# Moving weight loads, row loads, splits and sums to other places in a fused attention and expert kernel

## The chip, the cores and the metric

The kernel runs on one core of one Trainium2 chip. The metric is the time of one execution on the device, in microseconds (us).

## What is computed

A recurrent attention over 32 heads (4 batches of 8) gives x, 3072 rows of 384 numbers. Each row then goes to the best two of eight experts, weighted by its gate:

```python
for e in range(E):
    for k in range(2):
        mask = top2[:, k] == e
        if not mask.any():
            continue
        h = np.maximum(x[mask] @ w1[e], 0.0)
        out[mask] += top2_w[mask, k, None] * (h @ w2[e])
```

`w1[e]` is 384x1024 and `w2[e]` is 1024x384, all in 32-bit floats.

## The kernel before

**Attention and gating** come first, in six groups of 512 rows. Their steps and the steps of the first two experts are calls with names. The text `EMIT` sets the order in which the calls are written, and the table `ORDER` sets by hand the order of their instructions on each engine: PE (matmul), ACT, DVE, POOL, and SP, whose queue issues the plain DMAs. A token such as `load_w20.2` is the third instruction of one call on one engine. In names, `mm10_0_5` is the first product of the first expert, first half of its rows, sixth block of hidden units; `load_w10` and `load_w11` load the first weights of the first and of the second expert, `load_w20` the second weights of the first expert, `load_x1_0` the first half of the second expert's rows. At the end of gating each row is scattered by POOL into `xs`, a DRAM tensor with one stretch for each expert.

**The experts** are ranked by their number of rows. The largest two are computed in the hand-ordered part; the other six in a loop, `for e in range(2, E)`, where e is the rank. In the loop there is no table: the program text, a scheduler and the dependencies named `order` set the order, and SP's DMAs stay in the order of the text.

One expert's turn has these pieces. Half `w=0` has 256 to 320 rows ("narrow"), half `w=1` has 512 ("wide").

- `mm1(e, w)`: for each of eight blocks f of 128 hidden units, nine matmuls into one of four PSUM buffers `ph`. ACT then writes the rounded high part of relu (line 933, list `highs`), DVE the rest (line 936, list `lows`). We call these two the eviction of block f. A buffer is free after both.
- `mm2(e, w)`: hidden units times `w2` into one of two PSUM buffers `po`; DVE adds the weighted result to `ao` (line 980, list `kept`), POOL scatters `ao` into the output. For e of 2 to 5 the first half is computed turned (`mm2_turned`): it goes through the DRAM tensor `op`, comes back by a transposing DMA (`turn_back`, line 1001), and is added (`add_turned`, lines 1008 and 1011) in the turn of the next expert.
- Weights: a load into one of three `raw` buffers (lines 861 and 870), then a split in a high part by ACT and a low part by DVE (line 851). `w1` comes in three loads, `w2` in four; the fourth `w2` load needs a `raw` buffer that a split has emptied.
- Rows of the next expert: `load_x` brings them into `xga` (first half) and `xgb` (second), `x_G` reads out the gates on DVE, `x_P` copies the halves of each word apart on ACT (line 816) and stores them in `xp`, `x_L` reads them back with twelve transposing DMAs of SP (line 825), and `x_T` copies (DVE, line 910), rounds (ACT, line 913) and subtracts (DVE, line 914).
- `gather_o`: POOL reads the output rows into `ao` before they are added to.

The tile `xp0` serves both `x_P` of the first half and the turned product on its way to `op`; `xp1` serves `x_P` of the second half and the turned sums on their way back. An engine runs its instructions in their order: one that waits holds all behind it.

Of the kernel before, what the change touches and what calls it, by code (L numbers as in the profile page):

```python
# [71 lines left out]
    tr_unit22_0 p3q23_1 load_x1_0 sc_unit21_0 st_scale17 x_unit19 tr_unit22_1 sc_unit21_1 y_unit21 tr_unit23_0  # L72
    gdis4_3_4 sc_unit22_0 st_scale18 sc_unit22_1 tr_unit23_1 st_scale19 y_unit22 sc_unit23_0 load_v23 sc_unit23_1
    gscat4_3_4 glog5_0_3 x_unit20 gturn5_0_3 mm10_0_5 gsel5_0_3 mm10_0_6 y_unit23 gdis5_0_3 mm10_0_0 mm10_0_3 x_unit21
    mm10_0_7 mm10_0_4 close_q load_w20 load_w11 x_T1_0_0 glog5_3_4 x_T1_0_1 gturn5_3_4 x_unit22 gscat5_0_3 gsel5_3_4
    x_unit23 x_T1_0_2 gdis5_3_4 rank gscat5_3_4 x_G1_0 clear_out3 clear_mp mm20_0_0 mm20_0_1 mm20_0_2 mm11_0_0
    mm11_0_1 mm11_0_2 load_x0_1 mm11_0_3 mm11_0_4 mm11_0_5 mm11_0_6 x_G0_1 x_T0_1_0 x_T0_1_1 mm11_0_7 x_T0_1_2
    mm10_1_0 mm10_1_1 mm10_1_2 load_x1_1 x_P1_1 x_L1_1 mm10_1_3 mm10_1_4 mm10_1_5 mm10_1_6 mm10_1_7 ranked load_w12
    x_T1_1_0 load_x2_0 x_T1_1_1 mm20_1_3 mm20_1_4 x_G1_1 x_T1_1_2 x_P2_0 x_L2_0 x_G2_0 mm20_1_5 load_x2_1 mm20_1_6
    x_P2_1 x_L2_1 x_G2_1 load_w21 mm11_1_0 mm11_1_1 mm11_1_2 mm11_1_3 mm11_1_4 gather_o1 mm11_1_5 mm21_0_0 mm11_1_6  # L80
    mm21_0_1 mm11_1_7 x_T2_0_0 x_T2_0_1 x_T2_0_2 mm21_0_2 mm21_1_3 x_T2_1_0 x_T2_1_1 x_T2_1_2 mm21_1_4 mm21_1_5
    mm21_1_6
# [119 lines left out]
        gdis4_0_3.2 gdis4_0_3.1 sc_unit22_0.0 gsel4_3_4.16 gdis4_0_3.3 load_w20.0 sc_unit22_1.0 load_w20.2 st_upd15.0  # L202
        st_scale19.0 gdis4_3_4.0 gdis4_3_4.1 sc_unit23_1.0 sc_unit23_0.0 load_w20.1 gturn5_0_3.0 gsel5_0_3.0
        gsel5_0_3.1 gsel4_3_4.13 load_w20.3 gsel5_0_3.2 gsel5_0_3.3 mm10_0_5.0 gsel5_0_3.4 gsel5_0_3.5 gsel5_0_3.6
        mm10_0_5.1 gsel5_0_3.9 gsel4_3_4.14 gsel5_0_3.8 gsel5_0_3.7 gsel5_0_3.12 gsel5_0_3.11 mm10_0_6.0 mm10_0_6.1
        gsel5_0_3.14 gsel5_0_3.15 gsel5_0_3.10 gsel5_0_3.13 gsel5_0_3.16 gsel5_0_3.20 gdis4_3_4.2 mm10_0_0.0
        gsel4_3_4.15 gsel5_0_3.17 gdis4_3_4.3 gsel5_0_3.18 mm10_0_0.1 gdis5_0_3.0 gsel5_0_3.19 gdis5_0_3.2 mm10_0_3.0
        mm10_0_3.1 gdis5_0_3.3 gdis5_0_3.1 x_T1_0_0.0 mm10_0_7.0 gturn5_3_4.0 gsel5_3_4.0 x_T1_0_1.0 gsel5_3_4.1
        gsel5_3_4.2 gsel5_3_4.3 gsel5_3_4.4 gsel5_3_4.5 gsel5_3_4.6 mm10_0_7.1 mm10_0_4.0 gsel5_3_4.7 gsel5_3_4.10
        gsel5_3_4.8 mm10_0_4.1 gsel5_3_4.11 gsel5_3_4.9 gsel5_3_4.12 gsel5_3_4.13 load_w11.0 gsel5_3_4.14 gsel5_3_4.16  # L210
        x_T1_0_2.0 gsel5_3_4.15 rank.1 gdis5_3_4.0 gdis5_3_4.2 gdis5_3_4.3 clear_mp.0 clear_mp.4 load_w11.2 load_w11.1
        gdis5_3_4.1 rank.0 rank.2 clear_mp.3 clear_mp.2 clear_mp.1 clear_mp.5 rank.3 mm20_0_1.0 mm20_0_0.0 mm11_0_2.0
# [111 lines left out]
def kernel(  # L324
# [468 lines left out]
    def load_x(e, w, dst):  # L793
# [14 lines left out]
    XU = {}  # L808
    after = mybir.DependencyInfo(mybir.DependencyClass.NoSync, mybir.DependencyReason.DATA)

    def x_P(e, w):
# [3 lines left out]
        for i in range(len(js)):  # L815
            nc.scalar.copy(t[:, i], src_t[:, i, 0:DM].bitcast(U16).rearrange("p (d two) -> p two d", two=2))
# [450 lines left out]
    for e in range(2, E):  # L1267
# [5 lines left out]
        else:  # L1273
            for f2 in range(RAW):
                split_w2(f2)
# [206 lines left out]
```

## Time and profile before

| | |
|---|---|
| time, three runs | 667.25 us median (666.02 to 670.16) |
| the profiled execution | 667.93 us, its span 666.2 us |
| PE busy | 642.0 us, 96% of the span |
| DVE busy | 433.1 us, 65% |
| ACT busy | 366.7 us, 55% |
| POOL busy | 177.7 us, 27% |
| granted clock of PE, mean | 0.995 |

The span goes from the first to the last instruction that the profiler saw; the execution has 1.7 us around it. All durations below are from this one execution. Busy time of PE counts a matmul to its modelled end, so a busy PE may still be slower than its peak; idle time of PE is certain.

### The profile page before, as it was taken

The numbers are of one execution on the slowest core, as the hardware profiler recorded it, in microseconds if no ns is written. First come the engines' busy times: TensorE is split into PE (matmuls) and PEld (weight loads), VectorE is DVE, ScalarE is ACT, GpSimd is POOL, SyncE is SP. The second block draws the span as 40 slices with busy tenths as digits, with TensorE's granted clock in tenths as the row PEclk, the third lists the DMA queues.
The fourth block names the chain that finished last, engine by engine and source line by source line (L and its number), as shares of the span: only waits on it lengthen the run. The fifth ranks groups of instructions, "written<-read, shape, count | busy, mean of one in ns | idle before, by whom it ended". The sixth has DMA issues, their size and how long they took to land.

```text
span 666.2 us, 14314 instructions
## 1 busy us (share of the span) xinstructions
PE 642.0 (96%) x5511; PEld 568.9 (85%) x5514; DVE 433.1 (65%) x976; ACT 366.7 (55%) x609; POOL 177.7 (27%) x183
## 2 busy tenths in 40 slices
PE   7889999999999899999999999999998998999995
PEld 3467787878899799898998999999898898899894
DVE  6999999999999576455566167347427607827311
ACT  6999999999855452545237227326415515604200
POOL 3000000065524551036224023412411602523111
PEclk9999999999999999999999999999999999999998
DMA  6946756667595842686629467768766677772111
GB/s 236 302 136 165 214 148 225 207 212 234 184 276 175 295 178 99 241 242 175 180 85 341 77 192 240 184 176 267 174 163 216 185 185 206 216 196 84 45 37 36
DMA packets 117901, 123.75 MB, mean 186 GB/s; under 512 B 71498, under 2 KB 96992, under 8 KB 117824
## 3 DMA queue, kind: packets, MB, share of 16 engines
q1 hardware_dynamic: 108560, 95.27, 48.6%
q0 software_dynamic: 9264, 27.48, 12.8%
q8 instruction: 45, 0.74, 0.5%
q14 instruction: 32, 0.26, 0.1%
HBM read 70.11 MB, written 42.90 MB: 170 GB/s over the span
## 4 chain that ended last, share of the span: by engine, by line
PE 68%; ACT 10%; DMA 8%; SPq 7%; DVE 4%; issue 2%; POOL 0%; POOLq 0%; DVEq 0%; ACTq 0%
PE ph L931 21%; PE po L967 20%; SPq L825 5%; PE ptr L584 5%; PE psc L594 4%; PE po L992 3%; PE pY L643 2%; PE pY L645 2%; PE cum L534 2%; DMA xgb<-xs 2%; PE cum L561 2%; ACT t L468 2%; PE pG L606 2%; PE psc L931 2%; DMA op<-xp 2%
## 5 line engine op out<-in xcount | busy, mean ns | idle before, releaser
L931 PE MATMUL ph<-x,w1h 128*128 128x512 f32 (+4 forms) x720 | 185.2, 345 | 3.3 <-DVE h L936 3.2
L967 PE MATMUL po<-w2h,h 128*128 128x384 f32 x640 | 164.9, 335 | 0.8 <-DVE ao L980 0.8
L931 PEld LDWEIGHTS ph<-x,w1h 128*128 128x128 f32 x720 | 125.1, 188 | 19.2 <-DVE h L936 4.1
L952 POOL DMA_INDIRECT out_dram<-ao,ox x54 | 59.1, 1094 | 263.8 <-DVE ao L980 190.6
L931 PE MATMUL ph<-x,w1l 128*128 128x512 f32 (+4 forms) x360 | 124.0, 344 | 0.0
L967 PEld LDWEIGHTS po<-w2h,h 128*128 128x128 f32 x640 | 115.8, 188 | 1.7 <-DVE ao L980 1.4
L933 ACT ACTIVATE h<-ph 128x512 fp32r<-128x512 f32 (+4 forms) x120 | 60.0, 508 | 91.0 <-PE ph L931 78.5
L936 DVE SCALAR_TENSOR_TENSOR h<-ph,h 128x512 fp32r<-128x512 f32 (+5 forms) x128 | 68.5, 547 | 62.9 <-ACT h L933 62.6
L967 PE MATMUL po<-w2l,h 128*128 128x384 f32 x320 | 107.0, 334 | 0.0
L716 POOL DMA_INDIRECT xs<-xr,sl x48 | 58.3, 1215 | 178.0 <-DMA ecol<-es 129.4
L980 DVE SCALAR_TENSOR_TENSOR ao<-po,gw,ao 128x384 f32<-128x384 f32 (+1 forms) x42 | 25.7, 614 | 93.4 <-PE po L967 93.3
L931 PEld LDWEIGHTS ph<-x,w1l 128*128 128x128 f32 x360 | 67.6, 188 | 7.8 <-DVE w1l L851 0.2
L943 POOL DMA_INDIRECT ao<-out_dram,ox x47 | 52.4, 1115 | 32.6 <-issue 24.2
L967 PEld LDWEIGHTS po<-w2l,h 128*128 128x128 f32 x320 | 60.1, 188 | 0.2
L913 ACT CAST x<-xj 128x512 fp32r<-128x512 f32 (+4 forms) x39 | 20.6, 529 | 69.1 <-DVE xj L910 67.9
L914 DVE TENSOR_TENSOR x<-xj,x 128x512 fp32r<-128x512 f32 (+4 forms) x39 | 22.6, 578 | 31.0 <-ACT x L913 31.0
L594 PE MATMUL psc<-qT,kT 112*64 112x128 f32 (+1 forms) x768 | 38.9, 249 | 0.5 <-ACT kT L585 0.5
L594 PEld LDWEIGHTS psc<-qT,kT 112*64 112x64 f32 x768 | 35.8, 137 | 3.8 <-issue 2.6
L992 PE MATMUL po<-h,w2h 128*128 128x272 f32 (+2 forms) x192 | 38.7, 294 | 0.0
L645 PE MATMUL pY<-am,v 128*48 128x128 f32 x384 | 36.0, 273 | 0.2 <-DVE am L595 0.2
L595 DVE TENSOR_TENSOR am<-psc,mask 128x512 f32<-128x512 f32 x48 | 32.4, 681 | 4.0 <-PE psc L594 4.0
L851 DVE TENSOR_TENSOR w2l<-raw,w2h 128x768 fp32r<-128x768 f32 x32 | 30.3, 951 | 6.9 <-ACT w2h L851 6.9
(242 smaller groups left out, 1096.9 us busy)
## 6 DMA issues: line engine op xcount, KB each, us to landing
raw<-in_moe_w_dram SPq DMA_DIRECT2D x24, 512.0 KB
raw<-in_moe_w_dram SPq DMA_DIRECT2D x32, 384.0 KB
qk<-in_qk_dram SPq DMA_DIRECT2D x24, 384.0 KB
v<-in_v_dram SPq DMA_DIRECT2D x24, 288.0 KB
xgb<-xs SPq DMA_DIRECT2D x8, 800.0 KB
xp<-xp SPq DMA_DIRECT2D x7, 768.0 KB
re<-in_a_dram SPq DMA_DIRECT2D x12, 384.0 KB
im<-in_a_dram SPq DMA_DIRECT2D x12, 384.0 KB
```

The costliest lines, as they stand in the source:

```text
L584: nc.tensor.transpose(p[:, h, :], x[:, h, :, :].rearrange("p r x -> p (r x)")[:, 0:112], ident)
L594: nc.tensor.matmul(p[o:o + 64, j, z:], KT[n][:, h, z:z + 64], QT[n][:, h, z:], start=True, stop=True, skip_group_check=True)
L645: nc.tensor.matmul(o, V[n][:, H + h // 2 if h % 2 else h, :], AM[n][:, h, :], start=not g, stop=True, skip_group_check=True)
L716: d = nc.gpsimd.indirect_dma_start(out=xs, out_offset=bass.IndirectOffsetOnAxis(ap=sl[:, kk, b:b + 1], axis=0), in_=XR[g][:, lo + b, :], i ...
L825: nc.sync.dma_start(x[:, i, :], xp[e % 2, lo:lo + n, i * DM + kk * 128:i * DM + (kk + 1) * 128], transpose=True)
L931: nc.tensor.matmul(p[:, :n], W1[e, kk][i][:, f * 128:(f + 1) * 128], XW[w, kk][:, j, :], start=(c == 0), stop=(c == len(ms) - 1))
L933: highs.append(nc.scalar.activation(h[:, 0:n], p[:, :n], AF.Relu))
L936: d = nc.vector.scalar_tensor_tensor(h[:, dst:dst + b - a], p[:, a:b], 0.0, h[:, a:b].bitcast(F32), op0=OP.max, op1=OP.subtract)
L943: nc.gpsimd.indirect_dma_start(out=ao[j][0:w, :], out_offset=None, in_=out, in_offset=bass.IndirectOffsetOnAxis(ap=OX[e][0:w, j:j + 1], ax ...
L952: d = nc.gpsimd.indirect_dma_start(out=out, out_offset=bass.IndirectOffsetOnAxis(ap=OX[e][0:n, j:j + 1], axis=0), in_=a, in_offset=None, b ...
L967: nc.tensor.matmul(p[:, :DM], HT[w, f][i][:, o:o + 128], W2[f // 2][k2][:, f % 2, :], start=(m == 0), stop=(m == len(ms) - 1))
L992: nc.tensor.matmul(p[:, :n], W2[f // 2][k2][:, f % 2, kk * 128:(kk + 1) * 128], HT[0, f][i][:, 0:n], start=(m == 0), stop=(m == len(ms) - 1))
```

## The change

Three things change; the matmuls and their order on PE stay as they are.

1. **At the end of attention**, three of the four loads of the first expert's second weights (`load_w20_0_1_2`) stand on SP's queue ahead of two stores to `xd` and of the second expert's rows; the fourth (`load_w20_3`) stays behind the rows. The splits keep their places on ACT and DVE.
2. **Loads in the loop.** The next expert's rows are loaded ahead of the fourth `w2` load and of the `w1` loads. The store and the transposes of the first half are issued between `w1` loads, ahead of the second half's store.
3. **Work between evictions in the loop.** For e from 3 on, the first three `w2` splits move from the end of the turn before to places behind the second, fourth and sixth narrow eviction, the fourth behind the first wide one. `x_P` of the first half comes behind the sixth to eighth narrow eviction and of the second half behind the fourth wide one (for e=2 one copy behind each of the first four), the `w1` splits behind the fifth to seventh wide one. The last third of `x_T` (second half, last 128 columns) moves from the end of the turn before to behind the first narrow eviction. The turned sums come behind the first to third wide eviction.

The core of the diff (the table rows only rename `load_w20` except on SP):

```diff
@@ ORDER, SP
-        load_x0_0.0 load_x0_0.1 p322.2 p321.2 load_v20.0 load_v21.0 load_v22.0 p322.1 gscat3_0_4.0 gscat4_0_3.0
-        load_x1_0.0 load_x1_0.1 load_w20.0 load_w20.1 load_w20.2 load_v23.0 load_w20.3 load_w11.0 load_w11.1
+        load_x0_0.0 load_x0_0.1 p322.2 p321.2 load_v20.0 load_v21.0 load_v22.0 p322.1 load_w20_0_1_2.0
+        load_w20_0_1_2.1 load_w20_0_1_2.2 gscat3_0_4.0 gscat4_0_3.0 load_x1_0.0 load_x1_0.1 load_v23.0 load_w20_3.0
...
-    def x_P(e, w):
+    def x_P(e, w, part=None):
...
-        t = mt([128, len(js), 2, DM], U16, name=f"xp{w}")
-        for i in range(len(js)):
-            nc.scalar.copy(t[:, i], src_t[:, i, 0:DM].bitcast(U16).rearrange("p (d two) -> p two d", two=2))
-        nc.sync.dma_start(xp[e % 2, js[0] * 128:(js[-1] + 1) * 128].rearrange("(j p) r -> p j r", p=128),
+        if not part:
+            XP[w] = mt([128, len(js), 2, DM], U16, name=f"xp{w}")
+        t = XP[w]
+        for i in range(len(js)) if part is None else (part,):
+            d = nc.scalar.copy(t[:, i], src_t[:, i, 0:DM].bitcast(U16).rearrange("p (d two) -> p two d", two=2))
+            if e > 2:
+                tc.add_manual_dep(d.ins, highs[i - 3 if w == 0 else -1].ins.name, after, reason="order")
+        if part in (None, len(js) - 1):
+            nc.sync.dma_start(xp[e % 2, js[0] * 128:(js[-1] + 1) * 128].rearrange("(j p) r -> p j r", p=128),
...
+    def raw_w1(e, kk):
+        r = RW1[kk] = mt([128, FF], F32, name="raw", bufs=RAW)
+        nc.sync.dma_start(r, of(w1, e)[kk * 128:(kk + 1) * 128, :])
+
+    def split_w1(e, kk, behind=None):
+        W1[e, kk] = [mt([128, FF], F32R, name=f"w1{x}{kk}{e % 2}") for x in "hl"]
+        split(RW1[kk], *W1[e, kk], behind)
...
-    def load_w2(e):
-        for f2 in range(KF // 2):
+    def load_w2(e, fs=range(KF // 2)):
+        for f2 in fs:
...
-                tc.add_manual_dep(t.ins, kept[-1].ins.name, after, reason="order")
+                tc.add_manual_dep(t.ins, (lows[-KF] if (w, kk) == (1, KD - 1) else kept[-1]).ins.name, after, reason="order")
...
     def add_turned(e, y):
-        for j, first in zip(tiles_of(e, 0), lows[-3:] if e + 2 < E else lows[-6:]):
+        for j, first in zip(tiles_of(e, 0), lows[-KF:]):
...
-    at(P["w2"] + .5, load_w2, 0)
+    at(P["w2"] + .5, load_w2, 0, tuple(range(RAW)))
+    at(P["w2"] + .5, load_w2, 0, (RAW,))
...
         mm1(e, 0)
+        if more:
+            load_x(e + 1, 0, xga)
+            load_x(e + 1, 1, xgb)
         if e > 2:
+            x_T(e, 1, KD - 1)
+            for f2 in range(RAW):
+                split_w2(f2, 2 * f2 + 1 - KF)
             raw_w2(e, RAW)
-            split_w2(RAW, -4)
+        if more:
+            for kk in range(KD - 1):
+                raw_w1(e + 1, kk)
+            x_G(e + 1, 0)
+            x_P(e + 1, 0)
+        for f in range(KF):
+            mm1(e, 1, (f,))
+            if f == 0:
+                if e > 2:
+                    split_w2(RAW, -1)
+                if more:
+                    raw_w1(e + 1, KD - 1)
+                    x_L(e + 1, 0)
+                    x_G(e + 1, 1)
+            if more and f < len(JS[1]):
+                x_P(e + 1, 1, f)
+            if more and f == len(JS[1]) - 1:
+                x_L(e + 1, 1)
+            if more and f >= len(JS[1]) and f < len(JS[1]) + KD:
+                split_w1(e + 1, f - len(JS[1]), -1)
         if e - 1 in FLIP:
             add_turned(e - 1, y)
...
-                for w, kk in {3: ((0, 0), (0, 1)), 4: ((0, 2), (1, 0)), 5: ((1, 1),), 6: ((1, 2),)}[j]:
+                for w, kk in {3: ((0, 0), (0, 1)), 4: ((0, 2), (1, 0)), 5: ((1, 1),), 6: ()}[j]:
```

On SP's queue at the end of attention, in the kernel before (`xd` stores of two groups, the second expert's rows into `xga`, then the first expert's second weights; an ISA row sets the address):

```order
L713 DMA xd<-xr_2052 128x4x392
L713 DMA xd<-xr_2634 128x3x392
L796 ISA
L796 DMA xga_94<-xs 128x800
L798 ISA
L798 DMA xga_94<-xs 64x400
L870 ISA
L870 DMA raw_3722<-in_moe_w2_dram 128x2x384
```

Here the weights come last. The same place of SP's queue now:

```order
L882 DMA raw_3722<-in_moe_w2_dram 128x2x384
L882 ISA
L882 DMA raw_3728<-in_moe_w2_dram 128x2x384
L882 ISA
L882 DMA raw_3734<-in_moe_w2_dram 128x2x384
L714 DMA xd<-xr_2052 128x4x392
L714 DMA xd<-xr_2634 128x3x392
L797 ISA
L797 DMA xga_94<-xs 128x800
```

The three loads now stand ahead of the stores and rows.

On ACT, first product of expert e=5 (`h00` to `h07` are its narrow evictions, `h10` the first wide one; `w2h0` a split's high part, `x12` the last third of `x_T`, `xp0` a copy of `x_P`), in the kernel before:

```order
L851 CAST w2h2_6593<-raw_6352 128x768
L933 ACTIVATE h00_6597<-ph_6598 128x272
L913 CAST x12_6580<-xj_6581 128x512
L933 ACTIVATE h01_6610<-ph_6611 128x272
L816 COPY xp0_6875<-xga_94 128x768
L933 ACTIVATE h02_6623<-ph_6624 128x272
L816 COPY xp0_6875<-xga_94 128x768
L933 ACTIVATE h03_6636<-ph_6637 128x272
L933 ACTIVATE h04_6649<-ph_6650 128x272
L851 CAST w2h3_6703<-raw_6701 128x768
```

Here the first three splits are done ahead of the evictions, and the copies come early. The same place of ACT now:

```order
L949 ACTIVATE h01_6593<-ph_6594 128x272
L857 CAST w2h0_6691<-raw_6348 128x768
L929 CAST x12_6686<-xj_6687 128x512
L949 ACTIVATE h02_6606<-ph_6607 128x272
L949 ACTIVATE h03_6619<-ph_6620 128x272
L857 CAST w2h1_6695<-raw_6350 128x768
L949 ACTIVATE h04_6632<-ph_6633 128x272
L949 ACTIVATE h05_6645<-ph_6646 128x272
L857 CAST w2h2_6699<-raw_6352 128x768
L819 COPY xp0_6714<-xga_94 128x768
L949 ACTIVATE h06_6658<-ph_6659 128x272
L819 COPY xp0_6714<-xga_94 128x768
```

The copies from `xga` moved from behind the second narrow eviction to behind the sixth, the splits in among the evictions.

On SP's queue between the turn of e=4 and that of e=5 (`xp1` returns the turned product; `xga`, `xgb` are rows for e=6), in the kernel before:

```order
L1001 DMA_TRANSPOSE xp1_6436<-op 128x3x384 x2
L870 ISA
L870 DMA raw_6701<-in_moe_w2_dram 128x2x384
L796 ISA
L796 DMA xga_94<-xs 128x800
L805 ISA
L805 DMA xgb_3900<-xs 128x1600
```

Here the rows come behind the weights. The same place of SP's queue now:

```order
L1017 DMA_TRANSPOSE xp1_6436<-op 128x3x384 x2
L797 ISA
L797 DMA xga_94<-xs 128x800
L806 ISA
L806 DMA xgb_3900<-xs 128x1600
L882 ISA
L882 DMA raw_6703<-in_moe_w2_dram 128x2x384
```

The rows moved ahead of the fourth `w2` load.

## Rows read from the trace of the kernel before

**Rows 1.** Page, busy time: engine, us, share of the span, instructions.

```profile
PE 642.0 (96%) x5511; PEld 568.9 (85%) x5514; DVE 433.1 (65%) x976; ACT 366.7 (55%) x609; POOL 177.7 (27%) x183
```

**Rows 2.** Engines by stretch: stretch, length, busy us (instructions) of each, clock, DMA.

```profile
220.00:240.00 20.00, 17.84 (x210) 16.60 (x209) 12.66 (x56) 9.35 (x20) 10.07 (x9) 1.00 0.75 261
...
488.00:542.00 54.00, 51.86 (x314) 48.28 (x312) 28.07 (x51) 22.95 (x39) 15.41 (x14) 1.00 0.68 187
542.00:596.00 54.00, 52.10 (x299) 48.54 (x299) 29.41 (x54) 20.97 (x36) 16.30 (x15) 1.00 0.72 205
...
650.00:666.20 16.20, 8.02 (x47) 7.70 (x45) 1.59 (x3) 0.00 (x0) 2.92 (x3) 0.81 0.11 37
```

**Rows 3.** What PE waited for, 200 to 667 us: total, times, longest.

```profile
PE ph L931 <- DVE h L936: 3.2, 3, 1.3
PE cum L662 <- ACT xr L654: 1.3, 1, 1.3
PE cum L662 <- ACT xT L646: 0.8, 1, 0.8
PE po L967 <- DVE ao L980: 0.8, 2, 0.5
```

**Rows 4.** PE in order of time, 206 to 252 us: start, us, [idle before <- releaser].

```profile
225.93 0.41 PE L662 MATMUL cum<-xT,wg 128*32 128x128 f32 x4 [1.34 <-ACT xr L654]
227.16 1.06 PE L662 MATMUL cum<-xT,wg 128*32 128x128 f32 x20 [0.82 <-ACT xT L646]
```

**Rows 5.** ACT in order of time, 195 to 240 us.

```profile
224.66 0.83 ACT L851 CAST w2h<-raw 128x768 fp32r<-128x768 f32 x1 [2.66 <-DMA raw<-in_moe_w_dram]
```

**Rows 6.** SP's queue in order of time, 180 to 235 us.

```profile
198.53 13.14 SPq L713 DMA_DIRECT2D xd<-xr  x2
...
213.74 1.83 SPq L870 DMA_DIRECT2D raw<-in_moe_w_dram  x3
...
221.67 0.37 SPq L870 DMA_DIRECT2D raw<-in_moe_w_dram  x1
```

**Rows 7.** DVE in order of time, 195 to 252 us.

```profile
201.32 1.22 DVE L851 TENSOR_TENSOR w1l<-raw,w1h 128x1024 fp32r<-128x1024 f32 x1
```

**Rows 8.** ACT in order of time, 485 to 515 us.

```profile
494.24 0.83 ACT L816 COPY xp<-xga 128x768 uint16<-128x768 uint16 x1 [8.48 <-DMA op<-xp]
...
506.64 0.39 ACT L933 ACTIVATE h<-ph 128x272 fp32r<-128x272 f32 x1
509.63 0.83 ACT L816 COPY xp<-xga 128x768 uint16<-128x768 uint16 x1 [2.60 <-DMA xga<-xs]
```

**Rows 9.** PE in order of time, 488 to 512 us.

```profile
507.92 0.52 PE L931 MATMUL ph<-x,w1h 128*128 128x272 f32 x2 [1.03 <-DVE h L936]
```

**Rows 10.** SP's queue in order of time, 450 to 515 us.

```profile
494.28 2.85 SPq L1001 DMA_TRANSPOSE xp<-op  x2
503.37 0.39 SPq L870 DMA_DIRECT2D raw<-in_moe_w_dram  x1
503.95 0.36 SPq L796 DMA_DIRECT2D xga<-xs  x1
```

**Rows 11.** DVE in order of time, 485 to 515 us.

```profile
502.40 0.94 DVE L851 TENSOR_TENSOR w2l<-raw,w2h 128x768 fp32r<-128x768 f32 x1
```

**Rows 12.** Chain that ended last, whole span: start us, us, what.

```profile
381.64 16.65 PE po L967 x96
...
566.61 16.62 PE ph L931 x72
```

**Rows 13.** ACT in order of time, 270 to 345 us.

```profile
275.67 3.02 ACT L816 COPY xp<-xgb 128x768 uint16<-128x768 uint16 x4
```

**Rows 14.** POOL in order of time, 552 to 612 us.

```profile
576.00 1.07 POOL L943 DMA_INDIRECT ao<-out_dram,ox  x1 [2.54 <-issue]
```

**Rows 15.** DVE in order of time, 555 to 590 us.

```profile
571.72 0.60 DVE L1011 SCALAR_TENSOR_TENSOR ao<-xj,gw,ao 16x384 f32<-16x384 f32 x1
...
587.45 0.62 DVE L980 SCALAR_TENSOR_TENSOR ao<-po,gw,ao 128x384 f32<-128x384 f32 x1 [2.86 <-PE po L967]
```

More of the change, by code (lines that the diff above doesn't have):

```diff
@@ L71 @@
     mm10_0_1 st_scale16 y_unit20 tr_unit21_0 p3q21_1 mm10_0_2 tr_unit21_1 gdis4_0_3 gscat4_0_3 x_G0_0 p3q23_0
[L72 to L80, printed above, removed]
@@ L83 @@
+    mm21_0_0 mm11_1_6 mm21_0_1 mm11_1_7 x_T2_0_0 x_T2_0_1 x_T2_0_2 mm21_0_2 mm21_1_3 x_T2_1_0 x_T2_1_1 x_T2_1_2
+    mm21_1_4 mm21_1_5 mm21_1_6
 """
@@ L157 @@
+        x_P2_1.2 mm11_1_6.0 x_T2_0_0.0 x_T2_0_1.0 mm11_1_5.0 mm21_0_2.0 mm11_1_7.0 x_T2_0_2.0 x_T2_1_0.0 x_T2_1_1.0
+        x_T2_1_2.0
     """,
@@ L223 @@
+        x_T2_0_1.0 x_T2_0_1.1 mm21_0_1.0 mm11_1_2.0 mm11_1_6.0 mm21_0_2.0 mm11_1_5.0 x_G2_1.1 x_T2_0_2.0 x_T2_0_2.1
+        x_G2_1.2 mm11_1_7.0 mm21_0_2.1 x_T2_1_0.0 x_T2_1_0.1 x_T2_1_1.0 mm21_1_3.0 x_T2_1_1.1 mm21_1_4.0 mm21_1_5.0
+        x_T2_1_2.0 x_T2_1_2.1 mm21_1_6.0
     """,
@@ L859, in load_w1 @@
         for kk in range(KD):
-            r = mt([128, FF], F32, name="raw", bufs=RAW)
-            nc.sync.dma_start(r, of(w1, e)[kk * 128:(kk + 1) * 128, :])
-            W1[e, kk] = [mt([128, FF], F32R, name=f"w1{x}{kk}{e % 2}") for x in "hl"]
-            split(r, *W1[e, kk], 1 + 2 * kk - KF if e > 2 else None)
-    RW = {}
+            raw_w1(e, kk)
+            split_w1(e, kk)
+    RW, RW1 = {}, {}
     def raw_w2(e, f2):
@@ L889, in x_G @@
         t = chosen[:, 8 * E:(8 + len(js)) * E].rearrange("p (j e) -> p j e", e=E)
-        nc.vector.tensor_mul(t, src_t[:, 0:len(js), DM:DM + E], ONE[e][:, None, :].to_broadcast([128, len(js), E]))
+        d = nc.vector.tensor_mul(t, src_t[:, 0:len(js), DM:DM + E], ONE[e][:, None, :].to_broadcast([128, len(js), E]))
+        if e > 2:
+            tc.add_manual_dep(d.ins, lows[(-3, -1)[w]].ins.name, after, reason="order")
         nc.vector.tensor_reduce(GW[e][:, js[0]:js[-1] + 1], t, axis=AX.X, op=OP.add)
-        nc.vector.tensor_copy(OX[e][:, js[0]:js[-1] + 1], src_t[:, 0:len(js), RNO])
+        d = nc.vector.tensor_copy(OX[e][:, js[0]:js[-1] + 1], src_t[:, 0:len(js), RNO])
+        if e > 2:
+            tc.add_manual_dep(d.ins, lows[(-3, -1)[w]].ins.name, after, reason="order")
     def x_T(e, w, kk):
@@ L1270 @@
             held.close()
+        more = e + 1 < E
         if e == 2:
             load_w2(e)
-        else:
-            for f2 in range(RAW):
-                split_w2(f2)
-        if e == 2:
             for i in range(2):
@@ L1286 @@
         gather_o(e)
-        if e + 1 < E:
-            load_x(e + 1, 0, xga)
-            load_x(e + 1, 1, xgb)
-        mm1(e, 1)
-        if e + 1 < E:
-            load_w1(e + 1)
-            for w in range(2):
-                x_G(e + 1, w)
-                x_P(e + 1, w)
-            for w in range(2):
-                x_L(e + 1, w)
-        if e + 1 < E:
+        if more:
             for f2 in range(RAW):
```

84 lines of the change are left out of this document (44 added, 40 removed), and 2 rows, old and new, of the table PACE.

## The prediction

> **What bounds the kernel now.** I read the page first: PE is busy for 642.0 us, 96% of the span [rows 1]. All other engines are far below, and the change leaves every matmul in its place, so it can give back only time in which PE stands idle. The table of stretches says where that is: 2.16 us between 220 and 240 us (20.00 less 17.84), 2.14 us between 488 and 542, 1.90 us between 542 and 596, and 8.18 us at the end, where the last sums and scatters run out behind the last matmul [rows 2]. The rest of the idle time lies in the first 200 us, whose order the change doesn't touch. The list of PE's waits after 200 us names the same amount: 1.3 and 0.8 us in the gate's matmul, three waits of 3.2 us for a free `ph`, two of 0.8 us for a free `po`, 6.1 us in all [rows 3]. Up to 6.2 us is therefore the prize. Each wait has to be followed back to what made it.
>
> *The waits at 224 us.* PE's gate matmuls of line 662 wait 1.34 us for ACT's copy of `xr` and 0.82 us for its copy of `xT` [rows 4]. ACT is late because a split of `load_w20` stands ahead of those copies in its order and waits 2.66 us for its load, until 224.66 us [rows 5]. That load was issued between 213.74 and 215.57 us, since SP's queue sat in the two stores to `xd` from 198.53 to 211.67 us and then issued the second expert's rows [rows 6].
>
> *The waits for `ph`, e=5 and e=6.* PE waits 1.03 us at 507.92 us for an eviction [rows 9]. The evictions need ACT, and ACT, after its second narrow one at 506.64 us, stands 2.60 us in a copy from `xga` whose load is still on its way [rows 8]. SP issued that load at 503.95 us, right behind the fourth `w2` load at 503.37, although its queue had nothing to issue from 497.13 us on (494.28 plus 2.85) [rows 10]. A second wait in the same place and one of 1.3 us at e=6 make the 3.2 us.
>
> *The waits for `po`.* One of the three copies of `x_P` stands ahead of the casts of `x_T` on ACT and waits 8.48 us, until 494.24 us, since its tile `xp0` is still being stored to `op` [rows 8]. The casts, DVE's subtractions and DVE's eviction of `po` queue up behind it; PE loses 0.3 us there and 0.5 us in the next turn [rows 3].
>
> **The change part by part.**
>
> *Loads at the end of attention.* Three `raw` buffers are free when DVE's last split of the first expert's first weights ends, at 202.5 us (201.32 plus 1.22) [rows 7]; the last of the three loads is thus issued at about 202.6 us instead of 215.6. The casts stood between 9.1 and 10.9 us behind the issue of the late load (224.66 less 215.57 and less 213.74) [rows 5, 6]; even so the last would land at 213.5 us, over 6 us ahead of the first use. What the loads are moved past: the `xd` stores, which only the program's fallback reads, and the second expert's rows, which are issued right behind 211.67 us as before, since the second store sets that, and have fewer bytes beside them. ACT no longer waits, and both waits go: 2.16 us. Late next would be the fourth load, issued at 221.67 us when the first split has emptied its buffer [rows 6]; its cast stands behind the gate's next step and would come about 2 us earlier, some 6 us after the issue. With three loads fewer in the air I take no wait, and up to the whole 2.16 us as the bound.
>
> *Rows ahead of the fourth load.* SP can issue `xga` and `xgb` at 497.1 instead of 503.95 us [rows 10]. The load took 5.7 us (509.63 less 503.95) [rows 8, 10], so it lands near 503 us, when the first matmuls of e=5 have just begun, and its copies come only behind the sixth narrow eviction. ACT's wait is gone twice over. Given back: the three waits for `ph`, 3.15 us.
>
> *Copies behind evictions.* The copy that held the casts of `x_T` now stands in the next narrow half. Given back: the two waits for `po`, 0.8 us.
>
> *What takes their place.* A wide block of PE lasts 2.08 us (16.62 us for 72 matmuls, nine to a block) [rows 12]; a narrow one of 256 columns half of it, 1.04 us, an estimate. In a narrow half of 8.3 us ACT has eight evictions of 0.39 us, three copies and three splits of 0.83 us and one cast of about 0.6 us, 8.7 us by their spans, less by their overlap [rows 5, 8]; four `ph` buffers let it be three blocks late. In a wide half of 16.6 us the four copies in a row take 3.02 us [rows 13], one and a half blocks. DVE has three splits of 0.94 us [rows 11] and small steps beside eight evictions. The last third of `x_T` has 8.3 us until its first use and needs about 2 us. I price all of these at nothing; where the cover fails the price is the lag beyond three blocks.
>
> *The fourth `w2` load.* It needs the buffer of the first split, which now stands behind the second narrow eviction: two blocks, an eviction of 0.4, a cast of 0.83 and a subtraction of 0.94 us make 4.3 us after the start of the turn [rows 8, 11, 12]. Its cast stands behind the first wide eviction, at 10.4 us. So the load has 6.1 us, and 12.3 us before PE waits (three more buffers of 2.08 us). The nearest rows are 5.7 us and 9.1 to 10.9 us: ACT may wait, PE not. Price: nothing, with the slow bound as a rival.
>
> *Sums later.* The turned sums move about two wide blocks back, 4.2 us. In e=6 they ended at 572.32 us, the gathers began at 576.00 and the first sum that needs one came at 587.45 us [rows 14, 15]. Now the gathers begin near 580.2; one takes 1.07 us on POOL, so the first lands long ahead. Cost nothing, with some 5 us in hand.
>
> The `w1` splits end at the seventh wide block; their weights are first used a whole second product later. Transposes of the first half start earlier and free SP sooner. Both cost nothing.
>
> **The sum.** 667.93 us of the profiled execution, less 2.16, less 2.14, less 1.90, make 661.73 us. That execution lies 0.68 us over the median of 667.25, so I predict 661.05, given as 661.0 us.
>
> **Rivals.**
>
> *A. The first part is given back.* The gate's steps behind 226 us are a chain over PE, ACT and DVE, and its next link may wait for the fourth load or the second expert's weights. For it: that load's 9 to 11 us in the crowd [rows 5, 6]. Against it: three of the crowd are gone. Without the first term: 663.2 us.
>
> *B. The loop's waits are replaced.* ACT's and DVE's work in the narrow half fills nearly all of it, and e=6 and e=7 have the shortest blocks. If as much is lost there as now: 667.25 less 2.16, 665.1 us.
>
> *C. Slower: the fourth `w2` load comes late.* Its cast holds ACT, and behind it all wide evictions. It decides from 12.3 us after the issue. At 14 us PE loses 1.7 us in each of the five turns from e=3 to e=7, 8.5 us: 661.05 plus 8.5 is 669.6 us. Against it: no load in these rows took more than 10.9 us, and the rows are now out of its way.
>
> *D. More than the idle time.* A wide matmul takes 231 ns (16.62 us by 72) at a granted clock of 1.00, the upper level of 2.4 GHz, where 512 columns alone make 213 ns [rows 2, 12]. If the 17 ns were waits that the page counts as busy, and better placed evictions took them off, the 432 wide ones of the loop's first products (six turns of 72) would give 7.5 us more: 653.5 us. Against it: the second products, with few evictions, take 173 ns for 384 columns, 160 ns alone, so the excess goes with the matmul and not with evictions [rows 12]. The Trainium skill (TensorE: Matmul & The Clock Gate, Back-to-back issue gap) gives about 2.5 ns beyond the columns for matmuls in a row, which would make the excess a loss that can be won; this trace differs, with 13 to 17 ns whether evictions are many or few.
>
> *E. The order is not reached.* Splits could wait where the text puts them early. The instruction order shows them moved on SP, ACT and DVE, so I give this nothing.
>
> **How the numbers follow.** Both terms: 0.66, at 661.05 with 659.5 to 662.3 for itself, as runs of one kernel differ by about a microsecond. A: 0.13. B: 0.13. C: 0.05. D: 0.03. The range of 8 in 10 takes in A and B and leaves out C and D: 659.0 to 665.8. A measurement of this kernel can tell about 1% from no change, so faster means under 660.58 us: some third of the likeliest case and all of D, 0.25. Slower, over 673.9 us, needs C with loads of over 14 us: 0.03. Same: 0.72.
>
> **What would show it.** In the profile of the changed kernel PE should be busy in all of the stretch around 224 us, and the split of `load_w20` on ACT should have no idle time before it that a DMA ended. At the start of e=5 and e=6 ACT should have no wait for `xga`, PE none for `ph` or `po`, and SP's loads of `xga` should start some 7 us before the turn. PE's busy time should stay at 642 us with the span down to 660. Wrong would be: a wait of ACT for `raw` behind the first wide eviction with PE idle three blocks later (C), DVE evictions that lag in the narrow halves (B), or the same idle time a few microseconds on in the gate's chain (A).

## The result and the profile after

The changed kernel takes 659.88 us (median of six runs, 659.51 to 661.37) beside 666.40 us of the kernel before (six runs, 664.42 to 670.16). The ratio is 0.9901, with a 95% interval from 0.9873 to 0.9929. The forecast was 661.0 us in a range of 659.0 to 665.8.

The profiled execution after took 661.37 us, its span is 659.7 us. In the changed kernel line 816 has become 819, 851 is 857, 861 is 864, 870 is 882, 914 is 930, 931 is 947, 933 is 949, 936 is 952, 967 is 983 and 980 is 996. The page's line of busy time, as in [rows 1]:

```profile
PE 639.8 (97%) x5511; PEld 568.6 (86%) x5514; DVE 434.9 (66%) x976; ACT 365.8 (55%) x609; POOL 174.8 (27%) x183
```

The stretches of [rows 2] (columns as there):

```profile
220.00:240.00 20.00, 20.00 (x250) 18.82 (x251) 13.86 (x58) 10.37 (x21) 10.21 (x11) 1.00 0.66 223
...
488.00:542.00 54.00, 54.00 (x331) 51.14 (x329) 30.47 (x55) 23.58 (x41) 16.09 (x15) 1.00 0.76 214
542.00:596.00 54.00, 54.00 (x314) 51.17 (x314) 31.95 (x58) 21.64 (x38) 17.11 (x16) 1.00 0.69 197
...
650.00:659.70 9.70, 1.48 (x9) 1.16 (x7) 0.62 (x1) 0.00 (x0) 0.97 (x1) 0.75 0.10 34
```

PE is busy for all of the three stretches that lost time before, and the last 8.22 us without work are as they were (8.18). None of the waits of [rows 3] is left. A new one stands between 188 and 199 us, in a part whose order is unchanged and where PE was never idle before. Its row in the list of PE's waits (total, times, longest):

```profile
PE pY L646 <- DMA v<-in_v_dram: 1.5, 2, 1.0
```

Beside [rows 5, 6], SP's queue around the end of attention:

```profile
200.03 4.62 SPq L882 DMA_DIRECT2D raw<-in_moe_w_dram  x3
204.69 8.60 SPq L714 DMA_DIRECT2D xd<-xr  x2
...
222.85 0.39 SPq L882 DMA_DIRECT2D raw<-in_moe_w_dram  x1
```

and ACT:

```profile
223.52 0.82 ACT L857 CAST w2h<-raw 128x768 fp32r<-128x768 f32 x1
...
228.73 0.82 ACT L857 CAST w2h<-raw 128x768 fp32r<-128x768 f32 x1
```

The three loads are issued by 204.65 us, 11 us earlier than before. The cast that waited 2.66 us in [rows 5] is the one at 223.52 us now; neither it nor that of the fourth load, at 228.73 us, has idle time before it. Beside [rows 8, 10], SP's queue at e=5:

```profile
496.35 0.43 SPq L797 DMA_DIRECT2D xga<-xs  x1
...
505.15 0.38 SPq L882 DMA_DIRECT2D raw<-in_moe_w_dram  x1
```

and ACT in the same turn, which starts at 500.54 us:

```profile
508.59 0.83 ACT L819 COPY xp<-xga 128x768 uint16<-128x768 uint16 x1
...
512.43 0.82 ACT L857 CAST w2h<-raw 128x768 fp32r<-128x768 f32 x1
```

The rows are asked for 4.2 us ahead of the turn, the copies and the fourth cast start without a wait.

**Where the time came from.** Idle time alone does not give the difference: the span is 6.5 us shorter, and of that the waits of [rows 3] are 6.1 us, from which the new waits take 1.5. I therefore compared where the same matmuls start. The turns of e=4, 5 and 6, each from its first matmul to that of the next (stretch, length, PE busy, clock, DMA), before:

```profile
450.44:502.18 51.74, 51.46 (x314) 1.00 0.72 198
502.18:556.44 54.26, 51.93 (x314) 1.00 0.71 191
556.44:608.05 51.61, 50.18 (x289) 1.00 0.64 192
```

and after:

```profile
449.38:500.54 51.16, 51.16 (x313) 1.00 0.75 193
500.54:551.70 51.16, 51.16 (x313) 1.00 0.76 204
551.70:601.51 49.81, 49.81 (x289) 1.00 0.59 182
```

The lengths add up to 157.61 and 152.13 us. That is 5.48 us less, where 4.04 us were idle (157.61 less 153.57); the other 1.44 us vanished from time that was counted as busy. The same between two `pY` matmuls around the gate, first before:

```profile
221.28:231.48 10.20, 8.04 (x114) 1.00 0.86 297
```

and after:

```profile
222.90:230.47 7.57, 7.57 (x114) 1.00 0.81 237
```

Here 2.63 us went, of which 2.16 us were idle. PE's rows of before at one of the waits show where the difference hides ([rows 9] has the row between the first two):

```profile
506.60 0.29 PE L931 MATMUL ph<-x,w1l 128*128 128x272 f32 x1
...
508.28 0.29 PE L931 MATMUL ph<-x,w1l 128*128 128x272 f32 x1
508.41 0.42 PE L931 MATMUL ph<-x,w1h 128*128 128x272 f32 x2
508.66 0.29 PE L931 MATMUL ph<-x,w1l 128*128 128x272 f32 x1
```

A matmul is shown for 0.29 us, but the next one normally starts 0.13 us after it (508.28, 508.41). Ahead of the wait it doesn't, so 0.16 us of the stall are drawn as work; and the first pair behind the wait takes 0.36 us to the next start (507.92, 508.28) where a pair takes 0.25 (508.41, 508.66). The stall listed with 1.03 us cost 1.03 plus 0.16 plus 0.11, which is 1.30 us.

**What ended the waits for `ph`.** There are four `ph` buffers, so the fifth block of a turn has to wait until ACT and DVE have evicted the first. In the kernel before, DVE at e=5, then DVE, ACT and PE at e=6:

```profile
505.97 0.94 DVE L851 TENSOR_TENSOR w2l<-raw,w2h 128x768 fp32r<-128x768 f32 x1
506.83 0.68 DVE L914 TENSOR_TENSOR x<-xj,x 128x512 fp32r<-128x512 f32 x1
507.43 0.78 DVE L936 SCALAR_TENSOR_TENSOR h<-ph,h 128x272 fp32r<-128x272 f32 x2
...
510.79 0.44 DVE L936 SCALAR_TENSOR_TENSOR h<-ph,h 128x272 fp32r<-128x272 f32 x1 [0.76 <-ACT h L933]
...
561.66 0.74 DVE L936 SCALAR_TENSOR_TENSOR h<-ph,h 128x256 fp32r<-128x256 f32 x2
...
561.89 0.83 ACT L816 COPY xp<-xga 128x768 uint16<-128x768 uint16 x1 [0.64 <-DMA xga<-xs]
...
562.13 0.50 PE L931 MATMUL ph<-x,w1h 128*128 128x256 f32 x2 [1.30 <-DVE h L936]
```

The waits of 1.03 us (until 507.92 us) and of 1.30 us (until 562.13 us) end with DVE's first eviction of the turn. It came late because DVE had a split and the last third of `x_T` in front of it, left over from the turn before. ACT's copy from `xga` didn't make it late: that copy started at 509.63 us [rows 8], when the first of the two waits was over, and at 561.89 us, when DVE had already begun the eviction. Only the second wait at e=5, 0.82 us until 511.29 us, ends with an eviction that came late on ACT (510.79 us) behind this copy.

DVE's first eviction ended 5.7 and 5.6 us into the turns of e=5 and e=6, but 3.5, 3.4 and 3.4 us into those of e=3, e=4 and e=7, which have no wait. What sets e=5 and e=6 apart is the copy at the end of the turn before that waited for the `op` stores, until 494.24 us [rows 8] and in the next turn:

```profile
548.49 0.83 ACT L816 COPY xp<-xga 128x768 uint16<-128x768 uint16 x1 [8.64 <-DMA op<-xp]
```

`x_T` and the splits queued up behind it. In the changed kernel, DVE's first eviction at e=5 ends 2.2 us into the turn:

```profile
502.30 0.44 DVE L952 SCALAR_TENSOR_TENSOR h<-ph,h 128x272 fp32r<-128x272 f32 x1 [0.94 <-ACT h L949]
```

With the two waits for `po` (0.28 and 0.47 us) the backlog behind that one copy thus made 3.1 of the loop's 4.04 us of idle time, the loads of the rows the rest.

The whole account of the profiled executions, by starts of the same matmuls: 0.27 us less at the start, 1.87 us more at the two waits for `v`, 2.63 less at the gate, 5.5 less in the loop, 6.5 us in all.

### The profile page after: what moved, and what is told of

It is laid out like the page before. It is cut to its first block, busy times and chain, and to the rows that moved or that the text cites. A ratio compares the mean times of both kernels' runs of the same rounds, so it can differ in the third digit from the quotient of the medians.

```text
span 659.7 us, 14304 instructions
## 1 busy us (share of the span) xinstructions
PE 639.8 (97%) x5511; PEld 568.6 (86%) x5514; DVE 434.9 (66%) x976; ACT 365.8 (55%) x609; POOL 174.8 (27%) x183
## 4 chain that ended last, share of the span: by engine, by line
PE 78%; ACT 10%; DVE 6%; DMA 2%; issue 2%; SPq 1%; POOL 0%; POOLq 0%; DVEq 0%; ACTq 0%
PE ph L947 30%; PE po L983 25%; PE po L1008 6%; PE ptr L585 3%; ACT t L469 3%; PE psc L595 2%; PE pY L644 2%; PE psc L947 2%; PE pY L646 2%; DMA v<-in_v_dram 1%; PE cum L535 1%; PE cum L562 1%; ACT L468 1%; ACT qT L586 1%; ACT ee L469 1%
```

## The experiments

The eleven runs below were made on three chips, each beside the kernel before on the same chip. On the first (experiments 1 to 4) the kernel before took 667.5 us. On the other two (5, 7, 9 and the first run of 6; 8, 10 and the second run of 6) every kernel, the one before too (694.2 and 693.3 us), was some 27 us longer. In the profiles taken there the 27 us lie between 139 and 300 us; the kernel before has none from these chips. So these kernels are compared with each other, and by stretches behind 300 us.

**1. The loads at the end of attention alone.** The kernel before with the new tables and:

```diff
-    at(P["w2"] + .5, load_w2, 0)
+    at(P["w2"] + .5, load_w2, 0, tuple(range(RAW)))
+    at(P["w2"] + .5, load_w2, 0, (RAW,))
```

> The kernel before with only the early issue of the first expert's second weights. Theory (the two parts add up, and a stall costs a little more than the idle time listed for it): both gate waits at 224 us go, 2.16 us as listed and 2.6 us by PE's start times, about 663.8 us; the three waits for ph and the two for po stay. Rival A (the gate's chain gives the term back further on): the waits reappear within a few microseconds and the time stays at 666.4 us. Rival V (the waits for v between 185 and 200 us, seen only in the changed kernel, come with the early loads): they show here too, and the gain is about 0.8 us, 665.6 us.

Measured: 664.08 us, ratio 0.9947 (0.9928 to 0.9965). What PE waited for behind 200 us:

```profile
PE ph L932 <- DVE h L937: 3.3, 3, 1.3
PE po L968 <- DVE ao L981: 0.5, 1, 0.5
```

The gate's waits are gone and the loop's are there. By the starts of matmuls the gate is 2.63 us shorter, and nothing is given back behind it: rival A falls. There is no wait for `v`, so those don't come with the early loads.

**2. The loop alone.** The changed kernel with the old tables and the old line of experiment 1.

> The changed kernel with the old places at the end of attention, so only the loop's part. Theory: the gate waits of 1.3 and 0.8 us stay, the waits for ph and po are gone; the loop is 5.5 us shorter by PE's start times although 4.0 us of idle time were listed, so about 660.9 us; no waits for v. Rival (a stall costs what the list of waits says, and the rest of the changed kernel's gain came from elsewhere): the loop is 4.0 us shorter, 662.4 us. If the waits for v are a matter of the single execution, they may show here as well, at up to 1.9 us.

Measured: 663.29 us, ratio 0.9931 (0.9911 to 0.9952). The gate's two waits are PE's only ones behind 200 us, the second with 0.8 us as in [rows 3], the first:

```profile
PE cum L662 <- ACT xr L654: 1.2, 1, 1.2
```

The loop is 5.5 us shorter by starts, as in the changed kernel, but the time is 2.4 us above what I expected. By starts the gate is 1.7 us longer than in the profile of the kernel before. The stretch behind its waits (length, PE busy, granted clock, DMA) shows why:

```profile
224.00:228.00 4.00, 1.99 (x42) 1.00 0.66 237
228.00:232.00 4.00, 4.00 (x19) 0.57 0.90 267
```

while in the profiled execution of the kernel before the clock stayed up behind the same waits:

```profile
228.00:232.00 4.00, 4.00 (x37) 1.00 0.95 298
```

So this stall sometimes costs a second time, by a stretch near the lower level of the clock, 1.2 GHz. Experiments 1 and 2 take 3.4 and 4.2 us off the 667.5, together as much as kernels with both parts on this chip (8.4 us, below) within their intervals: the two parts add. The changed kernel itself was 6.5 us faster in its own comparison.

**3. Rows late.** The changed kernel with the next expert's rows behind the fourth `w2` load:

```diff
-        if more:
-            load_x(e + 1, 0, xga)
-            load_x(e + 1, 1, xgb)
         if e > 2:
...
             raw_w2(e, RAW)
         if more:
+            load_x(e + 1, 0, xga)
+            load_x(e + 1, 1, xgb)
```

> The changed kernel with the next expert's rows issued behind the fourth w2 load again; the copies keep their places behind the last narrow evictions. Theory (either half of that step is enough to remove the ph waits): ACT waits some 3 us for xga behind the seventh narrow eviction, PE none, since three blocks cover it; 660 us as the changed kernel, within 0.7 us. Rival (the early rows are what removes the waits): PE waits for ph come back at e=5 and e=6, 1 to 4 us in sum, 661 to 664 us.

Measured: 659.13 us, ratio 0.9871 (0.9850 to 0.9892); no wait of PE behind 200 us, turns as long as in the changed kernel to 0.01 us. ACT at e=5:

```profile
507.72 0.83 ACT L819 COPY xp<-xga 128x768 uint16<-128x768 uint16 x1 [0.23 <-DMA xga<-xs]
```

With the late copies the rows needn't be early. But ACT waited 0.23 us here and at most 1.33 in the other turns, not 3, as this load, issued at 504.13 us, was there after 3.6 us where [rows 8, 10] have 5.7; so the cover of three blocks wasn't put to the test.

**4. Both back, without a fixed place.** Experiment 3, and the copies need only be behind the second narrow eviction:

```diff
-                tc.add_manual_dep(d.ins, highs[i - 3 if w == 0 else -1].ins.name, after, reason="order")
+                tc.add_manual_dep(d.ins, highs[1 - KF if w == 0 else -1].ins.name, after, reason="order")
```

> The changed kernel with rows issued late and the copies allowed from the second narrow eviction on, as before: at e=5 and e=6 the first copy of xga stands behind the third narrow eviction. Theory: the load is issued near 505.5 us and lands 5.7 us later, ACT stands 6 to 7 us, PE covers 3.1 us of it; waits for ph of 3 to 5 us in each of the two turns, 666 to 670 us, slower than the changed kernel by 6 to 10 us. Rival (places don't matter, the gain came from the fewer transfers in the air): no wait for ph, 660 to 661 us.

Measured: 659.08 us, ratio 0.9876 (0.9857 to 0.9895), no wait for `ph`. My expectation was wrong because of the order: the copy that moved ahead is the third, which reads no loaded rows there, and the scheduler left the two that wait for the load behind the seventh and eighth eviction. The kernel tests nothing beyond experiment 3; the next two fix the places.

**5. Copies held early, rows early.** In the changed kernel, the first copy behind the second narrow eviction and the first cast, the second behind the third eviction, and in a loop all later evictions behind them:

```diff
+            if e > 3 and w == 0 and i < 2:
+                tc.add_manual_dep(d.ins, CAST[0].ins.name, after, reason="order")
+                for x in highs[i + 2 - KF:]:
+                    tc.add_manual_dep(x.ins, d.ins.name, after, reason="order")
             if e > 2:
-                tc.add_manual_dep(d.ins, highs[i - 3 if w == 0 else -1].ins.name, after, reason="order")
+                tc.add_manual_dep(d.ins, highs[(1 - KF, 2 - KF, -1)[i] if w == 0 else -1].ins.name, after, reason="order")
```

> The changed kernel with the first two copies of the next expert's rows held behind the second and third narrow eviction and ahead of the following one, in all four turns from e=3; the rows stay early. Theory (either half alone is enough): the rows land before the second eviction, ACT waits under 0.5 us, PE not at all, 659 to 660 us. Rival (the copies' late places are what removes the ph waits): PE waits of 1 us and more for ph in each of the four turns, 664 us or more.

Measured: 690.09 us, ratio 0.9929 (0.9900 to 0.9957), no wait of PE in the loop. ACT in the turn of e=5, which starts at 530.15 us:

```profile
534.16 0.83 ACT L819 COPY xp<-xga 128x768 uint16<-128x768 uint16 x1
```

The copy finds its rows there. With the early rows the copies needn't be late.

**6. Copies held early, rows late.** Both edits, of experiments 3 and 5; run twice.

> As the kernel with the held copies, and the rows issued behind the fourth w2 load as well, so both halves undone. Theory: the rows land some 9 us after the turn's start (4.4 to 5.7 us after the issue), ACT stands 5 to 6 us ahead of the third eviction, PE runs out of ph buffers at 6.2 us; it waits 3 to 5 us in each of the four turns, 672 to 680 us. Rival (the evictions' order doesn't decide, the gain came from elsewhere): no waits for ph, 659 to 660 us.

> The kernel with held copies and late rows once more, to see whether the fall of the granted clock behind its stalls (0.50 for some 3.6 us after 2.3 us without work) belongs to the chip of the earlier call. Theory: it doesn't, a stall of 2 us brings it on any chip, so four waits of about 2 us cost 3 to 4 us each, some 13 us over the changed kernel, ratio 1.006 to 1.012. Rival (it was that chip): the clock stays at 1.00 and each turn loses 2.0 to 2.6 us, 8 to 10 us over the changed kernel, ratio 1.000 to 1.004.

Measured: 701.76 and 701.60 us, ratios 1.0119 (1.0064 to 1.0173) and 1.0110 (1.0075 to 1.0145). In the first of the two, what PE and ACT waited for:

```profile
PE ph L952 <- DVE h L957: 8.1, 4, 2.3
...
ACT xp L819 <- DMA xga<-xs: 9.8, 2, 5.0
ACT xp L819 <- issue: 9.7, 2, 5.0
```

PE waits in all four turns: only with both halves undone does the load of the rows reach it. ACT stands about 5 us in the first copy in each turn; for two of them the trace names no releaser. These waits are of the kind of the 0.82 us at e=5 in the kernel before, made larger by the place in which the copies are held; they are not a return of the other two. They are listed with 1.75 to 2.31 us, less than the 3 to 5 I expected, because the built order has twelve matmuls of the turned product ahead of the block that waits, 1.5 us of work in the gap. The four turns nevertheless are 13.6 us longer than in experiment 5, where 8.1 are listed. The stretches around the third wait show the rest:

```profile
542.00:544.00 2.00, 0.44 (x4) 1.00 0.82 254
544.00:546.00 2.00, 1.25 (x6) 0.74 0.44 182
546.00:548.00 2.00, 2.00 (x11) 0.50 0.00 0
548.00:550.00 2.00, 2.00 (x11) 0.91 0.68 246
```

Behind 2.31 us without work the granted clock is 0.50 and comes back after some 4 us; that turn lost 4.0 us. The fourth wait, of 1.75 us, left the clock at 1.00, and its turn lost 2.0. In the second run all four waits were between 1.97 and 2.07 us, and all four turns lost 3.7 to 3.9 us. The two runs are from two chips, so the fall in the loop doesn't belong to one of them. Both are chips on which every kernel was longer; on the first chip no run has such stalls in the loop, but experiment 2 shows the fall there at the gate.

**7. The third copy free.** The changed kernel, with the third copy without its place where it reads no loaded rows:

```diff
-            if e > 2:
+            if e > 2 and (w or i < 2 or REST[e]):
```

> The changed kernel, with the third copy of the rows free of its place where it reads no loaded rows (e=6 and e=7), so that it stands ahead of the casts of x_T at the end of the turns e=4 and e=5, as before. Theory: it waits there for the op stores again, and the two waits for po return, 0.8 us as listed, 1.3 us by PE's start times: about 1.3 us over the changed kernel, 660 to 661 us. Rival (the po waits were the doing of the last third of x_T, which has left that stretch): no po wait, 659 to 660 us.

Measured: 688.44 us, ratio 0.9873 (0.9796 to 0.9951), four runs from 680.87 to 690.71 us; the time can't tell 1.3 us, the profile has to. ACT at the end of e=4:

```profile
521.89 0.83 ACT L819 COPY xp<-xga 128x768 uint16<-128x768 uint16 x1 [8.42 <-DMA op<-xp]
```

and PE:

```profile
525.55 0.44 PE L983 MATMUL po<-w2h,h 128*128 128x384 f32 x1 [0.24 <-DVE ao L996]
```

The wait for the `op` stores is back in both turns, the wait for `po` in one: the turn of e=4 is 0.51 us longer, as before (0.59), that of e=5 isn't. At e=5 the copy was free after 7.55 us, before after 8.64, and the remaining lag did not reach PE. The copy is thus the cause of the waits for `po`, and its wait lies at the edge of PE's cover. No wait for `ph` came back with it. DVE's first eviction of e=5, whose turn starts at 529.82 us:

```profile
532.00 0.43 DVE L952 SCALAR_TENSOR_TENSOR h<-ph,h 128x272 fp32r<-128x272 f32 x1
```

It ends 2.6 us into the turn, 0.4 us later than in the changed kernel: with the splits and the last third of `x_T` between the evictions, the backlog behind the copy no longer holds the first eviction up for long.

**8. Sums, gathers and the last third of `x_T` in their old places.**

```diff
-                tc.add_manual_dep(t.ins, (lows[-KF] if (w, kk) == (1, KD - 1) else kept[-1]).ins.name, after, reason="order")
+                tc.add_manual_dep(t.ins, kept[-1].ins.name, after, reason="order")
...
-        for j, first in zip(tiles_of(e, 0), lows[-KF:]):
+        for j, first in zip(tiles_of(e, 0), lows[-3:] if e + 2 < E else lows[-6:]):
...
-            x_T(e, 1, KD - 1)
...
+        if e - 1 in FLIP:
+            add_turned(e - 1, y)
+        gather_o(e)
         for f in range(KF):
             mm1(e, 1, (f,))
...
-        if e - 1 in FLIP:
-            add_turned(e - 1, y)
-        gather_o(e)
...
-                for w, kk in {3: ((0, 0), (0, 1)), 4: ((0, 2), (1, 0)), 5: ((1, 1),), 6: ()}[j]:
+                for w, kk in {3: ((0, 0), (0, 1)), 4: ((0, 2), (1, 0)), 5: ((1, 1),), 6: ((1, 2),)}[j]:
```

> The changed kernel with the turned sums and the gathers issued ahead of the wide half again and the last third of x_T in its old place at the end of the turn. Theory (both moves were priced at nothing): the same time as the changed kernel within 0.7 us, no wait of PE after 240 us. Rival (these moves freed DVE in the narrow half): waits for ph of 1 us and more at e=5 and e=6.

Measured: 688.00 us, ratio 0.9911 (0.9877 to 0.9946), beside 688.59 of the changed kernel on the same chip. Each turn of the loop is as long as there to 0.01 us, and PE waits for nothing in it. These moves are worth nothing, as priced.

**9. The fourth `w2` load late.** In the changed kernel it waits for the first wide eviction, and its cast stands ahead of the second; the `w1` loads move behind it.

```diff
+        if late is not None:
+            tc.add_manual_dep(d.ins, highs[late].ins.name, later, reason="late")
...
-            raw_w2(e, RAW)
...
+            if f and e > 2:
+                tc.add_manual_dep(highs[-1].ins, cast.ins.name, after, reason="order")
             if f == 0:
                 if e > 2:
-                    split_w2(RAW, -1)
+                    raw_w2(e, RAW, -1)
+                    cast = split_w2(RAW, -1)[0]
```

> The changed kernel with the fourth w2 load issued only when the first wide eviction is done, 6.4 us later than in its profile, its cast held ahead of the second wide eviction, and the loads behind it on SP moved along. Rival C of the prediction (the load decides once it lands more than 12.3 us after the old issue): ACT waits 4 to 7 us for raw and PE 0 to 1.6 us for ph in each of the five turns from e=3, 659 to 668 us, decided by whether the load takes more or less than 5.9 us. If PE waited with a shorter load, the cover of three blocks would have been counted too long; if a load over 7 us cost nothing, too short.

Measured: 689.94 us, ratio 0.9947 (0.9912 to 0.9982). At e=5, which starts at 527.68 us, SP and then ACT:

```profile
539.70 0.38 SPq L883 DMA_DIRECT2D raw<-in_moe_w_dram  x1
...
543.78 0.84 ACT L857 CAST w2h<-raw 128x768 fp32r<-128x768 f32 x1 [4.11 <-DMA raw<-in_moe_w_dram]
```

ACT waited 4.11 us, until 16.1 us into the turn, and PE not at all. In the five turns ACT waited 20.9 us in all; where its wait was longest, 5.3 us at e=6, the cast started 16.6 us into the turn and PE waited 0.2 us for `ph`. By starts the turns are 1.4 us longer than in experiment 5: 0.5 us at that wait, 0.9 in two second products, for which I have no cause. The prediction's point for rival C is 4.3 plus 12.3, 16.6 us into the turn: a cast at 16.1 us cost nothing at e=5, one at 16.6 us cost 0.5 us at e=6, so the cover was counted rightly to about half a microsecond, and rather too long.

**10. The changed kernel again.**

> The changed kernel once more, word for word, beside the kernel before on the chip of this call. Theory (the 1.5 us of waits for v belong to the one profiled execution and not to the change): PE's start times show the gate 2.6 us and the loop 5.5 us shorter, no waits for v, a ratio near 0.988 as with the kernels that have the rows late. Rival (they come with this order of loads): the waits for v are there again, ratio 0.990 to 0.991.

Measured: 688.59 us, ratio 0.9915 (0.9886 to 0.9943). No wait for `v`, and the loop's turns are as in the first profile to 0.01 us. But the stretch in which `v` was late is here among those that were longer (length, PE busy, granted clock, DMA):

```profile
190.00:200.00 10.00, 7.39 (x108) 0.83 1.01 299
```

PE reaches the matmuls on `v` later in this run, so it can't tell alone. The profiles of experiments 1, 3 and 4 have the same order up to 225 us on the first chip, and no wait for `v` either. I take the 1.87 us for a matter of the one execution, not of the change. That the ratio of the changed kernel lies over those of experiments 3 and 4 (0.9901 to 0.9871 and 0.9876, with intervals that overlap) stays unexplained; no instruction order that differs between them cost or gave time in any profile.

## Why the prediction was right

- **The waits at 224 us (2.16 us).** Right in cause: the loads issued early let ACT cast without a wait, both waits went, nothing came back (experiment 1). Wrong in size: 2.63 us by starts, and more in an execution in which the clock falls behind the stall (experiment 2).
- **The waits for `ph` (3.15 us).** They went, but for the larger part not for the reason given; that the whole term came out is luck there. The prediction lays them to ACT's wait for the rows. Of the 3.15 us only 0.82 ended behind it. The other 2.33 us ended with DVE's first eviction of the turn, late behind `x_T` and the splits, which the copy that waited for the `op` stores had held up; the prediction uses this copy for the waits for `po` alone. Two moves freed DVE, that of the copy and that of the splits and of `x_T`'s last third. With the copy back (experiment 7) the other move suffices; e=3, e=4 and e=7 of the kernel before have the old splits without the copy and no wait, but no run puts the splits back alone. For the 0.82 us, "ACT's wait is gone twice over" holds: no wait for the rows reaches PE with either half alone (experiments 3 and 5), and one does with both undone (6).
- **The waits for `po` (0.8 us).** Right: the copy that waited for the `op` stores is the cause (experiment 7), though one of the two waits depends on how long that store takes.
- **The size of the loop's term.** 4.04 us predicted, 5.48 measured. The mis-sized step is that the change "can give back only time in which PE stands idle", so that "up to 6.2 us is therefore the prize": 8.1 us were, since a listed stall leaves out 0.1 to 0.4 us that stand as busy time around it. For the same reason "PE's busy time should stay at 642 us" failed: it is 639.8.
- **The sum.** Predicted for the profiled execution 661.73 us, measured 661.37. That it is closer than its parts is luck: the terms were 1.9 us too small, and this execution lost 1.87 us at `v`. The median of 659.88 us lies 1.2 us under the forecast, the side on which the terms were too small. It also lies under 660.58 us, which the prediction called faster and gave 0.25; against the 666.40 us of all six runs before, the gain is 1.0%.
- **What was priced at nothing.** The new places on ACT and DVE, the fourth load, the sums, the last third of `x_T`: no wait of PE behind 200 us, and experiments 8 and 9 show the covers. But the places of the splits and of `x_T`'s last third belong to the second of the two moves that freed DVE.
- **A sign that was misstated.** The loads of `xga` should "start some 7 us before the turn"; they start 4.2 us before it. By the prediction's own numbers they would start 7 us earlier than before, which is 5 us ahead of the turn (497.1 to 502.18).
- **Rivals.** A fell with experiment 1, B with the three full turns above. C fell on size: in experiment 9 the load was there 4.1 us after its issue, and even 16.1 us into the turn cost nothing. D fell: the 25.48 us of the two halves of e=4's first product, in which no wait stood before, are 25.49 us after, so better placed evictions don't make a matmul shorter. The second products after, 96 matmuls of 384 columns in 16.65 us, still take 173 ns with 160 for the columns. The Trainium skill (TensorE: Matmul & The Clock Gate, Back-to-back issue gap) gives about 2.5 ns beyond the columns for an isolated matmul and sets a stream of weight loads and matmuls apart from it. This trace is such a stream and takes 13 ns beyond them, so the 2.5 ns is no measure of what it could win back.

## What to carry to other kernels

Where one engine is busy for 96% of the span, list its few idle stretches, follow each to the instruction that stood in front of the one that was needed, and move that instruction or its load; their sum was here a lower bound of the gain. Check the times on the way: an instruction that is released only after the stall is over can't have caused it, however long it waited, and the engine that the stall's row names (here DVE) is the one whose order to read first. To see the gain itself compare the starts of the same matmuls in two traces, not busy or idle time. If a wait is removed by two changes at once, undo them one by one and together, with the places held fast, since a scheduler may else quietly keep the good order.

## What was not expected of the hardware

- A stall costs more than its listed idle time: 0.27 us more for one of 1.03 us, from how the last matmul before it is drawn and from a slower first pair behind it.
- Behind stalls of 1.95 to 2.31 us the granted clock fell to 0.50 for some 4 us, behind one of 1.75 us it stayed at 1.00 (experiment 6); each turn with a fall lost 3.7 to 4.0 us, the other 2.0. Behind the gate's two waits it fell in one execution (0.57, waits of 2.0 us in sum, experiment 2) and not in another (1.00, 2.2 us, the kernel before).
- On two of the three chips all kernels were some 27 us longer, the kernel before too. In the changed kernel's profile there, PE between 139 and 270 us stands again and again for about 0.5 us in steps for which the trace names no releaser, with a lower clock behind them. What these are no view shows. The loop's turns were the same to 0.01 us. One of the steps:

```profile
189.83 0.26 PE L607 MATMUL pG<-v,kh 128*48 128x48 f32 x2 [0.48 <-issue]
```
